# Moving, splitting and re-sharing the side jobs of a fused convolution and gated feed-forward kernel

## The chip, the cores and the metric

The kernel runs on one core of one Trainium2 chip. The metric is device time in microseconds (us): the median over runs of the whole program. Each set of runs of a kernel was made beside runs of the kernel before on the same chip. Profile spans are about 1.8 us shorter than the time of the same run.

The engines are TensorE (PE; its weight loads are PEld), VectorE (DVE), ScalarE (ACT), GpSimd (POOL) and the sync engine (SP), whose queue issues most of the transfers.

## The reference

```python
# attention part: weights w = softmax(weight) over 7 taps, one row for each of 8 heads of 24 channels
out[b, s, h] = sum_k w[h, k] * x[b, s - 6 + k, h]      # x: 8 x 4096 x 192, zeros before s = 0
# feed-forward part on the 32768 rows of out
g = out @ w_gate                                       # 192 x 1536
y = (silu(g) * (out @ w_val)) @ w_out                  # 1536 x 192
```

All inputs and the output are float32; the kernel works in fp16 with float32 sums.

## The kernel before

The program is one loop of 768 steps. Twelve steps make a block of 512 rows, four blocks (48 steps) a unit. The scheduler does not reorder within an engine: `seq` chains each engine's instructions in the order of their emission.

A step makes 512 rows of one 128-wide slice of gate and of val, each in its own bank of PSUM (the tiles from `ppool`, which the matmuls write). The banks come from rings of three, that is, three banks used in turn:

```python
def gate_val(n):
    g = ppool.tile([P, TB], fp32, tag="gate", ...)      # bufs=3
    v = ppool.tile([P, TB], fp32, tag="val", ...)       # bufs=3
    ...                                                 # three pairs of 64-row matmuls (PE)
    silu[n] = seq(nc.scalar.activation(sg, g, AF.Silu)).ins     # ACT
    seq(nc.vector.tensor_tensor(hj, sg, v, op=ALU.mult))        # DVE: h
```

At steps 1, 4, 7 and 10 of a block 12, 24 or 36 `down` matmuls on finished h follow. The convolution is made in two ways. Unit 1 and the even units from 2 on are convolved on PE by band matmuls (`conv_half`), at two steps of the unit before (10 and 22; 25 and 31 in unit 0), with banks from the same gate and val rings:

```python
for hp in (2 * hh, 2 * hh + 1):
    banks = [ppool.tile([P, TB], fp32, tag=tag, name="cv") for tag in ("gate", "val")]
    ...                                                 # 16 matmuls into them
```

Odd units from 3 on ("pooled" units) are convolved tap by tap in channel-major form, beside PE: six jobs a unit, each with seven taps, done in slots at steps 1, 7 and 10 of a block.

```python
ON_DVE, ON_ACT, ON_POOL = (0, 1), (2, 3, 4), (5, 6)
def step(a):                       # three slots a job
    if a < len(ON_DVE):
        on_dve(ON_DVE[a])          # total = x_k * tap + (0 or total)
    on_act(ON_ACT[a])              # part = x_k * tap on ACT; then total += part on POOL
    if a == len(ON_ACT) - 1:
        for k in ON_POOL:
            on_pool(k)             # POOL: piece = x_k * tap (tensor_scalar); total += piece
```

The x of these jobs is transposed by DMAs on the sync queue. Their taps per channel come from a small computation at step 23: iota on POOL, two small operations on DVE for each of two selectors (`pick`), then matmuls into gate banks (`ctap`). One more transfer matters later: for the band matmuls of unit 2, `dup_x` copies the lower rows of `x16` after step 37, on the same sync queue.

## Time and profile before

| | |
|---|---|
| median of three runs | 792.34 us (791.21 to 792.58) |
| span of the profiled run | 788.7 us |
| PE, DVE, ACT, POOL busy | 99%, 80%, 74%, 57% |
| a block far from the start | 11.73 us, with a band convolution 12.4 us |
| unit 0 (48 steps) by the starts of its gate matmuls | 60.46 us |

PE is never idle for more than a fraction of a microsecond except in unit 0 and at its border. The lines are in the prediction. A line of a timeline reads: start, duration, engine, source line, operation, output and inputs, shapes; a bracket at the end has the engine's idle time before it and what ended it. Source lines shift with the edit: in the changed kernel L767 is gate and val, L776 the silu, L778 h, L793 the down matmuls, L668 DVE's taps, L649 POOL's multiply, L634 its adds.

### The profile page before, as it was taken

How to read it: one execution, taken by the hardware profiler on the slowest of the kernel's cores; microseconds unless marked ns; L12 is line 12 of the kernel's file. 1: busy time of each engine (PE TensorE's matmuls, PEld its weight loads, DVE VectorE, ACT ScalarE, POOL GpSimd, SP SyncE). 2: the span in 40 equal slices, each digit the busy share in tenths (PEclk: the TensorE clock that was granted, in tenths of full speed). 3: DMA queues.
4: the chain of work that ended last, by engine and by line, in shares of the span. 5: the costliest groups of instructions: out<-in, count | busy, mean ns of one | idle time of the engine just before them, and what ended most of it. 6: DMA issues, size and time to landing. Idle time of an engine off the chain costs nothing.

```text
span 788.7 us, 28107 instructions
## 1 busy us (share of the span) xinstructions
PE 778.3 (99%) x11563; PEld 600.3 (76%) x11563; DVE 627.3 (80%) x988; ACT 584.7 (74%) x1010; POOL 453.3 (57%) x375
## 2 busy tenths in 40 slices
PE   8898999999999999999999999999999999999998
PEld 5665678886788767887678876888678886788886
DVE  7666888688887888778897788877888788897775
ACT  6566778678777787777787687777787777786664
POOL 8204669455793658926689166873669546684000
PEclk9999999999999999999999999999999999999999
DMA  9996668653585444853557625674257652531111
GB/s 144 152 165 130 136 134 149 136 109 80 111 151 124 94 108 102 168 118 62 129 116 135 137 63 118 129 152 110 56 134 135 145 117 59 119 93 44 42 42 42
DMA packets 175970, 88.49 MB, mean 112 GB/s; under 512 B 115898, under 2 KB 175170, under 8 KB 175170
## 3 DMA queue, kind: packets, MB, share of 16 engines
q1 hardware_dynamic: 147634, 69.57, 38.3%
q0 software_dynamic: 28208, 17.13, 16.4%
q8 instruction: 90, 1.47, 0.8%
q14 instruction: 38, 0.31, 0.1%
HBM read 34.26 MB, written 39.37 MB: 93 GB/s over the span
## 4 chain that ended last, share of the span: by engine, by line
PE 96%; SPq 1%; ACT 1%; DVE 0%; DMA 0%; issue 0%; ACTq 0%
PE gate L740 51%; PE acc L766 32%; PE val L740 11%; PE cv L462 1%; SPq L498 1%; PE warm L841 1%; SPq L520 0%; PE turn L431 0%; DMA x<-xs 0%; PE cv L373 0%; ACT sig L749 0%; PE acc L787 0%; DVE h L751 0%; ACT tme L391 0%; ACT wide L331 0%
## 5 line engine op out<-in xcount | busy, mean ns | idle before, releaser
L751 DVE TENSOR_TENSOR h<-sig,val 128x512 f16<-128x512 f16 x768 | 503.5, 686 | 144.9 <-PE val L740 93.6
L749 ACT ACTIVATE sig<-gate 128x512 f16<-128x512 f32 x768 | 458.2, 597 | 176.1 <-PE val L740 104.0
L740 PEld LDWEIGHTS <-w 64*128 64x128 f16 x4608 | 321.8, 110 | 125.4 <-issue 2.9
L766 PEld LDWEIGHTS <-h 64*128 64x128 f16 x6096 | 275.8, 94 | 45.7 <-issue 4.0
L766 PE MATMUL acc<-wo,h 64*128 64x192 f16 x6096 | 306.1, 243 | 2.1 <-ACT sig L749 2.1
L740 PE MATMUL val<-xc,w 64*128 64x512 f16 x1296 | 306.9, 378 | 0.0
L740 PE MATMUL gate<-xc,w 64*128 64x512 f16 x1296 | 306.9, 378 | 0.0
L636 POOL TENSOR_TENSOR total<-total,part 128x512 f32<-128x512 f32 x126 | 160.1, 1270 | 225.9 <-DVE total L619 174.1
L740 PE MATMUL val<-pxc,w 64*128 64x512 f16 x1008 | 236.6, 376 | 0.0
L740 PE MATMUL gate<-pxc,w 64*128 64x512 f16 x1008 | 236.6, 376 | 0.0
L649 POOL TENSOR_SCALAR piece<-x,tap_c 128x512 f32<-128x512 f16 x84 | 137.9, 1641 | 0.0
L643 ACT ACTIVATE part<-x,tap_c 128x512 f32<-128x512 f16 x126 | 89.9, 714 | 3.7 <-DMA x<-xs 3.1
L636 POOL TENSOR_TENSOR total<-total,piece 128x512 f32<-128x512 f32 x42 | 54.2, 1290 | 3.5
L619 DVE SCALAR_TENSOR_TENSOR total<-x,tap_c,fill 128x512 f32<-128x512 f16 x42 | 41.1, 979 | 2.4 <-DMA x<-xs 2.4
L636 POOL TENSOR_TENSOR pxc<-total,piece 128x512 f16<-128x512 f32 x28 | 36.1, 1288 | 2.3
L825 DVE COPY o_sb<-acc 128x384 f32<-128x384 f32 x63 | 34.6, 549 | 0.0
L619 DVE SCALAR_TENSOR_TENSOR total<-x,tap_c,total 128x512 f32<-128x512 f16 x42 | 31.4, 748 | 3.5 <-POOL total L636 3.5
L824 ACT COPY o_sb<-acc 128x384 f32<-128x384 f32 x63 | 30.2, 479 | 0.1
L98 POOL DMA_DIRECT2D x<-in_x_dram x25 | 19.8, 800 | 13.3 <-ACT sig L749 13.1
L479 ACT CAST tm<-cv 128x480 f16<-128x480 f32 x32 | 16.3, 562 | 11.8 <-PE cv L462 11.8
L479 DVE CAST tm<-cv 128x480 f16<-128x480 f32 x32 | 19.6, 652 | 1.2
L490 POOL COPY tm<-tm 128x1280 f16<-128x1280 f16 x8 | 10.0, 1249 | 17.3 <-DVE tm L479 9.1
(68 smaller groups left out, 101.0 us busy)
## 6 DMA issues: line engine op xcount, KB each, us to landing
out_dram<-o_sb SPq DMA_DIRECT2D x63, 384.0 KB
scr<-tm SPq DMA_DIRECT2D x56, 130.0 KB
x<-x SPq DMA_DIRECT2D x14, 480.0 KB
xs<-in_x_dram POOLq DMA_DIRECT2D x7, 774.0 KB, 7.3
x<-in_x_dram POOLq DMA_DIRECT2D x11, 480.0 KB, 7.8
pxc<-pxc SPq DMA_DIRECT2D x56, 64.0 KB
pxc<-y SPq DMA_DIRECT2D x56, 64.0 KB
x<-in_x_dram POOLq DMA_DIRECT2D x7, 468.0 KB, 6.0
```

Source lines behind the costliest of these rows:

```text
L98: nc.gpsimd.dma_start(out=t[p0 + i0 : p0 + i1, w0 - at : w1 - at, :], in_=bass.AP(tensor=x_flat.tensor, offset=(t0 + size * w0 - pad + i0) ...
L479: eng(tm[u][:, NG * r : NG * r + NG, 2 * grp * hp : 2 * grp * hp + 2 * grp].rearrange("p g (t e) -> p g t e", t=2), banks[r][:, 0 : 2 * w] ...
L619: nc.vector.scalar_tensor_tensor(total.rearrange("p (s e) -> p s e", s=SUBS) if k == 0 else total, shifted(k).rearrange("p (s e) -> p s e" ...
L636: nc.gpsimd.tensor_tensor(dst if k == K - 1 else total, total, part, op=ALU.add)
L643: seq(nc.scalar.activation(part, shifted(k), AF.Copy, scale=tap[:, k : k + 1]))
L649: nc.gpsimd.tensor_scalar(part, shifted(k), scalar1=tap[:, k : k + 1], scalar2=None, op0=ALU.mult,)
L740: nc.tensor.matmul(o, w16[m][p0 : p0 + Q, k, e::E], xc[b][k][p0 : p0 + Q, 0:TB], start=(k == 0), stop=(k == SL - 1),)
L749: silu[n] = seq(nc.scalar.activation(sg, g, AF.Silu)).ins
L751: seq(nc.vector.tensor_tensor(hj, sg, v, op=ALU.mult))
L766: nc.tensor.matmul(acc[b][bank][:, s, :], hj[p0 : p0 + Q, ts(2 * bank + s, P)], wo16[p0 : p0 + Q, j, :], start=(not second and j == 0 and ...
L824: seq(nc.scalar.copy(o_sb[:, 0:2, :], acc[b][0]))
L825: seq(nc.vector.tensor_copy(o_sb[:, 2:4, :], acc[b][1]))
```

## The change

Its intent is to take the side jobs out of PE's way at the start of the program and to balance them better. It has these parts:

1. **Taps in two steps.** The selectors are made after step 24, the `ctap` matmuls after step 33.
2. **First jobs later.** A pooled unit's jobs are queued 95 steps ahead of it (103 before), those of the first one 86 ahead.
3. **New shares.** Jobs alternate two and three taps on DVE (three and two on ACT). Each slot takes one DVE tap and one ACT tap, each from its own list, and POOL's adds of a job start only when all of its DVE taps have been issued.
4. **POOL multiplies by broadcast taps**, as a two-input operation.
5. More buffers for some tiles, fewer for others, and the halves of the tiles are placed later.

```diff
-    def make_channel_taps():
+    def make_picks():
 ...
+    def make_channel_taps():
+        for name in pick:
             bank = ppool.tile([P, TB], fp32, tag="gate", name="ctap")
 ...
-    ON_DVE, ON_ACT, ON_POOL = (0, 1), (2, 3, 4), (5, 6)
+    SHARES = (
+        ((0, 1), (2, 3, 4), (5, 6)),
+        ((0, 1, 2), (3, 4), (5, 6)),
+    )
 ...
+        def proceed():
+            if job["dve"]:
+                return
+            while job["parts"]:
+                add(*job["parts"].pop(0))
+            if job["act"]:
+                return
+            for k in pool_taps:
+                part = cpool.tile([P, TB], fp32, tag="piece", name="piece", bufs=2)
+                seq(nc.gpsimd.tensor_tensor(part, shifted(k),
+                        job["tap"][:, k : k + 1].to_broadcast([P, TB]), op=ALU.mult))
+                add(part, k)
 ...
-        plan.setdefault(s0 - 103, []).append(
-            lambda: pending.extend((v, *job) for job in jobs)
-        )
+        plan.setdefault(s0 - (86 if v == POOLED[0] else 95), []).append(lambda: queue_jobs(v))
 ...
     def pooled_work(n, room):
+        if room:
+            if on_dve:
+                on_dve.pop(0)()
+            if on_act:
+                on_act.pop(0)()
 ...
-        if n == 23:
+        if n == 24:
+            make_picks()
+        if n == 33:
             make_channel_taps()
```

More of the change, by code (lines that the diff above doesn't have):

```diff
@@ L532 @@
     taps = {}
-    def make_channel_taps():
+    pick = {}
+    def make_picks():
         for name, first, rows in (("c01", 0, P), ("c2", P, Q)):
@@ L546, in make_channel_taps @@
             seq(nc.vector.tensor_single_scalar(low, which, 0, op=ALU.is_ge))
-            pick = small(f"pick_{name}", [H, P], fp16)
+            pick[name] = small(f"pick_{name}", [H, P], fp16)
             seq(
                 nc.vector.scalar_tensor_tensor(
-                    pick, which, float(grp), low, op0=ALU.is_lt, op1=ALU.mult
+                    pick[name], which, float(grp), low, op0=ALU.is_lt, op1=ALU.mult
                 )
             )
+    def make_channel_taps():
+        for name in pick:
             bank = ppool.tile([P, TB], fp32, tag="gate", name="ctap")
@@ L556, in make_channel_taps @@
                     nc.tensor.matmul(
-                        bank[:, 0:K], pick, split[:, a, 0:K, 0],
+                        bank[:, 0:K], pick[name], split[:, a, 0:K, 0],
                         start=(a == 0), stop=(a == 1),
@@ L591, in turn_x @@
         tag = f"x{at // Q}"
-        t = cpool.tile([P, TB + XP], fp16, tag=tag, name=tag, bufs=4)
+        t = cpool.tile([P, TB + XP], fp16, tag=tag, name=tag, bufs=6)
         seq(nc.sync.dma_start_transpose(out=t, in_=rows[:, at : at + P]))
@@ L597, in join_x @@
         seq(nc.sync.dma_start(out=x12[u, i + 2][0:Q], in_=x12[u, i][Q:P]))
-    ON_DVE, ON_ACT, ON_POOL = (0, 1), (2, 3, 4), (5, 6)
-    def conv_job(u, what, i):
-        if what == "pair":
-            dst = y2[u, i] = cpool.tile([P, TB], fp16, tag="y2", name="y2", bufs=4)
-            src, tap = x12[u, i + 2], taps["c2"]
-        else:
-            t = cpool.tile([P, XW], fp16, tag="pxc0", name="pxc0", bufs=6)
-            xc[UB * u + i] = [t]
-            dst = t[:, 0:TB]
-            src, tap = x01[u, i], taps["c01"]
-        total = cpool.tile([P, TB], fp32, tag="total", name="total", bufs=3)
-        at = XP - pad
-        def shifted(k):
-            return src[:, at + k : at + k + TB]
-        def on_dve(k):
-            zero = fill.unsqueeze(1).to_broadcast([P, SUBS, P])
+    SHARES = (
+        ((0, 1), (2, 3, 4), (5, 6)),
+        ((0, 1, 2), (3, 4), (5, 6)),
+    )
@@ new lines, with conv_job, open_job, add @@
+    on_dve = []
+    on_act = []
+    finished = {}
+    started = []
+    def conv_job(n_job, u, what, i):
+        dve_taps, act_taps, pool_taps = SHARES[n_job % len(SHARES)]
+        job = {"dve": len(dve_taps), "act": len(act_taps), "parts": []}
+        at = XP - pad
+        def open_job():
+            if what == "pair":
+                y2[u, i] = cpool.tile([P, TB], fp16, tag="y2", name="y2", bufs=4)
+                job.update(dst=y2[u, i], src=x12[u, i + 2], tap=taps["c2"])
+            else:
+                t = cpool.tile([P, XW], fp16, tag="pxc0", name="pxc0", bufs=8)
+                xc[UB * u + i] = [t]
+                job.update(dst=t[:, 0:TB], src=x01[u, i], tap=taps["c01"])
+            job["total"] = cpool.tile([P, TB], fp32, tag="total", name="total", bufs=4)
+        def shifted(k):
+            return job["src"][:, at + k : at + k + TB]
+        def add(part, k):
+            total = job["total"]
+            seq(
+                nc.gpsimd.tensor_tensor(
+                    job["dst"] if k == K - 1 else total, total, part, op=ALU.add
+                )
+            )
+        def proceed():
[7 more added lines that the diff above has]
+                part = cpool.tile([P, TB], fp32, tag="piece", name="piece", bufs=2)
+                seq(
+                    nc.gpsimd.tensor_tensor(
+                        part,
+                        shifted(k),
+                        job["tap"][:, k : k + 1].to_broadcast([P, TB]),
+                        op=ALU.mult,
+                    )
+                )
+                add(part, k)
+            finished[u, what, i] = True
+        def dve_step(k):
+            if "total" not in job:
+                open_job()
+            total, x_k, other = job["total"], shifted(k), job["total"]
+            if k == 0:
+                total = total.rearrange("p (s e) -> p s e", s=SUBS)
+                x_k = x_k.rearrange("p (s e) -> p s e", s=SUBS)
+                other = fill.unsqueeze(1).to_broadcast([P, SUBS, P])
@@ L618, in on_dve @@
             seq(
                 nc.vector.scalar_tensor_tensor(
-                    total.rearrange("p (s e) -> p s e", s=SUBS) if k == 0 else total,
-                    shifted(k).rearrange("p (s e) -> p s e", s=SUBS)
-                    if k == 0
-                    else shifted(k),
-                    tap[:, k : k + 1],
-                    zero if k == 0 else total,
-                    op0=ALU.mult,
-                    op1=ALU.add,
-                )
-            )
-        def part_tile(name):
-            return cpool.tile([P, TB], fp32, tag=name, name=name, bufs=4)
@@ L634, in add @@
-        def add(part, k):
-            seq(
-                nc.gpsimd.tensor_tensor(
-                    dst if k == K - 1 else total, total, part, op=ALU.add
-                )
-            )
-        def on_act(k):
-            part = part_tile("part")
-            seq(nc.scalar.activation(part, shifted(k), AF.Copy, scale=tap[:, k : k + 1]))
-            add(part, k)
-        def on_pool(k):
-            part = part_tile("piece")
-            seq(
-                nc.gpsimd.tensor_scalar(
-                    part, shifted(k), scalar1=tap[:, k : k + 1], scalar2=None,
-                    op0=ALU.mult,
-                )
-            )
-            add(part, k)
@@ L656, in step, with act_step @@
-        def step(a):
-            if a < len(ON_DVE):
-                on_dve(ON_DVE[a])
-            on_act(ON_ACT[a])
-            if a == len(ON_ACT) - 1:
-                for k in ON_POOL:
-                    on_pool(k)
-        return [lambda a=a: step(a) for a in range(len(ON_ACT))]
+                    total, x_k, job["tap"][:, k : k + 1], other,
+                    op0=ALU.mult, op1=ALU.add,
+                )
+            )
+            job["dve"] -= 1
+            proceed()
+        def act_step(k):
+            if "total" not in job:
+                open_job()
+            part = cpool.tile([P, TB], fp32, tag="part", name="part", bufs=6)
+            seq(
+                nc.scalar.activation(
+                    part, shifted(k), AF.Copy, scale=job["tap"][:, k : k + 1]
+                )
+            )
+            job["act"] -= 1
+            job["parts"].append((part, k))
+            proceed()
@@ L666, in place @@
+        on_dve.extend(lambda k=k: dve_step(k) for k in dve_taps)
+        on_act.extend(lambda k=k: act_step(k) for k in act_taps)
     def place(u, i):
@@ L669, in place @@
             xc[b].append(
-                cpool.tile([P, XW], fp16, tag=f"pxc{k}", name=f"pxc{k}", bufs=6)
+                cpool.tile([P, XW], fp16, tag=f"pxc{k}", name=f"pxc{k}", bufs=4)
             )
@@ L685, with queue_jobs @@
     plan = {}
-    pending = []
-    started = []
-    finished = set()
+    jobs_made = []
     placing = []
+    def queue_jobs(u):
+        for what, i in (
+            ("block", 0), ("pair", 0), ("block", 1), ("pair", 1),
+            ("block", 2), ("block", 3),
+        ):
+            conv_job(len(jobs_made), u, what, i)
+            jobs_made.append((u, what, i))
+        placing.extend((u, i) for i in range(UB))
     def planned(v):
@@ L700, in planned @@
             plan.setdefault(s0 + off, []).append(lambda i=i: join_x(v, i))
-        jobs = [("block", 0), ("pair", 0), ("block", 1), ("pair", 1)]
-        jobs += [("block", 2), ("block", 3)]
-        plan.setdefault(s0 - 103, []).append(
-            lambda: pending.extend((v, *job) for job in jobs)
-        )
-    def pooled_work(n, room):
-        while room:
-            if not started:
-                if not pending:
-                    break
-                u, what, i = pending.pop(0)
-                started.append((u, what, i, conv_job(u, what, i)))
-            u, what, i, steps = started[0]
-            steps.pop(0)()
-            room -= 1
-            if not steps:
-                started.pop()
-                finished.add((u, what, i))
-                for q in range(UB):
-                    need = {(u, "block", q), (u, "pair", q % 2)}
-                    if need <= finished and (u, what, i) in need:
-                        placing.append((n + 14, u, q))
-        while placing and placing[0][0] <= n:
-            _, u, q = placing.pop(0)
-            place(u, q)
+        plan.setdefault(s0 - (86 if v == POOLED[0] else 95), []).append(lambda: queue_jobs(v))
+    def pooled_work(n, room):
+        if room:
[3 more added lines that the diff above has]
+                on_act.pop(0)()
+        while placing:
+            u, i = placing[0]
+            need = (u, "block", i), (u, "pair", i % 2)
+            for job in need:
+                if finished.get(job) is True:
+                    finished[job] = n
+            if not all(job in finished for job in need):
+                break
+            if n < max(max(finished[job] for job in need) + 12, ustep * u + NCH * i - 16):
+                break
+            placing.pop(0)
+            place(u, i)
     hbuf = {}
@@ L895 @@
             job()
-        pooled_work(n, 0 if work else {1: 1, 7: 1, 10: 1}.get(j, 0))
+        pooled_work(n, j in (1, 7, 10) and not work)
         if u + 1 < NU and not pooled(u + 1):
```

## The prediction

> **What bounds the kernel now.** I read the page first. It names TensorE:
>
> ```profile
> PE 778.3 (99%) x11563; PEld 600.3 (76%) x11563; DVE 627.3 (80%) x988; ACT 584.7 (74%) x1010; POOL 453.3 (57%) x375
> ...
> PE 96%; SPq 1%; ACT 1%; DVE 0%; DMA 0%; issue 0%; ACTq 0%
> ```
>
> A busy PE is not proof of a PE at its peak, since the ends of matmuls are modelled. So I compared starts. The program has 768 steps (three gate/val matmul pairs, then a silu on ScalarE and a product h on VectorE); twelve make a block, 48 a unit. From the starts of h, every block from 84 us on takes 11.73 us, or 12.4 us in the two blocks of a unit in which TensorE also makes a convolution, until the last. Pairs start 0.215 us apart. The change removes and adds no matmul, so in this stretch nothing can be gained. Unit 0 and its border alone hold waits, and the table of busy times by stretch shows them:
>
> ```profile
> 35.95:39.37 3.42, 1.33 (x18) 0.62 (x16) 1.61 (x6) 0.76 (x2) 1.03 (x3) 1.00 0.99 102
> 39.37:42.78 3.41, 3.41 (x24) 1.55 (x24) 0.80 (x2) 1.36 (x3) 0.00 (x0) 0.50 1.71 128
> 63.25:66.67 3.42, 1.32 (x24) 0.81 (x22) 1.47 (x3) 1.95 (x4) 1.04 (x1) 1.00 0.51 112
> 66.67:70.08 3.41, 3.41 (x34) 2.26 (x30) 1.83 (x3) 1.18 (x3) 1.48 (x2) 0.50 0.64 86
> 551.83:563.56 11.73, 11.73 (x197) 8.51 (x194) 10.24 (x16) 9.18 (x16) 7.42 (x6) 1.00 0.28 54
> ```
>
> After the window come its length, then the busy time of PE, PEld, DVE, ACT and POOL; the third number from the end is the granted clock. Twice PE is busy for only 1.3 of 3.4 us, and twice the next 3.41 us run at clock 0.50. Each stop thus costs its idle time and half of a 3.41 us window, 1.7 us, on top. The last line is one steady block: VectorE has 1.5 us of slack in it.
>
> The first stop, from the timeline (start, duration, engine; in brackets the idle time before and its cause):
>
> ```profile
> 36.46 0.38 PE L740 MATMUL val<-xc,w 64*128 64x512 f16 x1
> ...
> 37.50 0.69 DVE L751 TENSOR_TENSOR h<-sig,val 128x512 f16<-128x512 f16 x1 [1.45 <-ACT sig L749]
> ...
> 38.34 0.28 DVE L549 SCALAR_TENSOR_TENSOR pick_c<-which_c,low_c 8x128 f16<-8x128 int32 x1
> ...
> 38.68 0.21 PE L556 MATMUL ctap<-split,pick_c 8*128 8x7 f16 x2 [1.85 <-DVE pick_c L549]
> ...
> 39.27 0.59 PE L740 MATMUL gate<-xc,w 64*128 64x512 f16 x1
> ```
>
> The ctap matmuls stand in PE's order behind step 23, but need selectors (pick) that VectorE makes only after h of step 23. The second stop:
>
> ```profile
> 63.50 0.38 PE L740 MATMUL val<-xc,w 64*128 64x512 f16 x1
> 64.72 0.72 ACT L643 ACTIVATE part<-x,tap_c 128x512 f32<-128x512 f16 x1 [3.14 <-DMA x<-xs]
> ...
> 65.35 1.55 ACT L749 ACTIVATE sig<-gate 128x512 f16<-128x512 f32 x3
> ...
> 65.98 2.45 PE L766 MATMUL acc<-wo,h 64*128 64x192 f16 x36 [2.10 <-ACT sig L749]
> ```
>
> The first channel-major job is queued at step 43, before its transposed x has landed. ScalarE runs in order, so the next silu sits behind the tap, and PE behind the silu.
>
> [...] Durations are minimum/median/maximum:
>
> ```profile
> L619 DVE SCALAR_TENSOR_TENSOR total<-x,tap_c,fill x42: 744/747/1409, 64.7 to 703.5; 128x512 f32<-128x512 f16 x42
> L619 DVE SCALAR_TENSOR_TENSOR total<-x,tap_c,total x42: 744/748/753, 67.8 to 708.9; 128x512 f32<-128x512 f16 x42
> ```
>
> First taps are 0.75 us or, 15 times, 1.39 to 1.41. Second taps are never slowed, because in this kernel GpSimd waits for them. One slow one:
>
> ```profile
> 584.43 1.27 POOL L636 TENSOR_TENSOR total<-total,piece 128x512 f32<-128x512 f32 x1
> ...
> 584.86 1.39 DVE L619 SCALAR_TENSOR_TENSOR total<-x,tap_c,fill 128x512 f32<-128x512 f16 x1
> ...
> 585.67 2.00 POOL L649 TENSOR_SCALAR piece<-x,tap_c 128x512 f32<-128x512 f16 x1
> ...
> 586.17 1.27 DVE L751 TENSOR_TENSOR h<-sig,val 128x512 f16<-128x512 f16 x2
> ...
> 586.90 0.37 PE L740 MATMUL val<-pxc,w 64*128 64x512 f16 x1
> ```
>
> The tap met an add with 0.84 us to go and lost 0.65 us; the next GpSimd multiply (usually 1.56) was held in turn. That h ends at 586.84 and the val matmul that needs its bank starts at 586.90, barely 0.05 us late and with no loss of pace: in this place (a tap after a step of remainder 1 in its block) 1.40 us is just what PE does not feel. [...] the adds here take 1.27. I take 1.27 for the multiply by broadcast taps; no run shows it yet.
>
> **The change, part by part.**
>
> *Taps in two steps.* From the start of step 23 (36.02) to that of step 26 (43.91) go 7.89 us. Unhindered, two steps of 0.65 and one with a convolution (2.40, as at step 31) are 3.70, so the stop costs 4.19. It does not vanish whole. Selectors now come after h of step 24: four small operations, together 0.95 us by their starts (38.10 to about 39.05). In step 25 two convolution pairs take two of the three gate and val banks, so val of step 26 needs the bank of h of step 25. That h would end at about 39.5 and now ends at about 40.4, against a PE ready at 39.7: 0.7 lost. At step 33 the two ctap banks take the same ring: gate of step 34 needs the bank of step 33, whose silu ends 0.79 after PE has finished step 33 (52.13 against 51.34 in the trace), plus a signal of 0.05: 0.84 lost. Neither leaves a window mostly idle, so I expect no clock drop. Net: 4.19 - 0.70 - 0.84 = 2.65 gained.
>
> *First jobs later.* Steps 46 to 49 take 7.37 us (63.07 to 70.44) where 2.13 + 0.65 + 0.65 = 3.43 would do: 3.94. The first job now waits for step 58, which itself holds a convolution, so really step 61. The x tile landed at 64.7; step 61 starts about 77. I expect all 3.94.
>
> *Two and three taps in turn.* Each slot (steps 1, 7 and 10 of a block) now has one VectorE and one ScalarE tap, so six jobs need 15 slots, not 18. VectorE gains 21 taps of 0.75 or more (105 for 84), ScalarE loses 21 of 0.71, GpSimd 21 adds of 1.27. A steady block with three taps costs VectorE, back to back, 12 x 0.60 + 0.53 + 3 x 0.75 = 10.0 us; with every tap at 1.40 it is 11.9 against 11.73. So the sum fits unless all are blocked. The local limit is the slot at step 1. Taps no longer wait for GpSimd's adds, so more of them meet GpSimd busy. Counting slots, about two of the step-1 slots of a unit fall in a busy stretch, 14 in seven units. A tap that meets an add at a random point waits up to about 1.07 us, 0.42 over the limit at worst; averaged over the 1.27 us this is about 0.1, and with lag carried from the slot before I take 0.15: 14 x 0.15 = 2 lost.
>
> *GpSimd.* Multiplies go from 1.64 mean to about 1.27: 84 x 0.37 = 31 us less work, all beside PE. More tile buffers and later placing take waits from queues that PE does not wait for.
>
> Sum: 792.3 - 2.65 - 3.94 + 2 = 787.7. The new slots were presumably tuned by someone who looked at the clock, so I lean a little lower: 787.0.
>
> **The rivals.**
> 1. *Contention decides.* GpSimd's stream is now all two-input work, and phases repeat from unit to unit, so a bad phase at step 1 repeats seven or fourteen times: 14 x 0.42 = 6 us, or 792; with lag over whole stretches, 35 blocks x 0.3 = 10 us, or 796. For it: the lines at 584.43. Against: the 1.5 us of slack.
> 2. *The transfers become the bound.* Without the stops PE reaches unit 1 some 6 us sooner. Its first x comes by the sync queue (last transpose issued at 60.8, landing near 63.4), which starts after the convolution of step 31 and so moves 3.5 us forward: near 60. Step 48 would start at 69.5 - 6.3 = 63.2. It holds by 3 us; if the queue did not move at all, 0.2 us and a little more would be lost, near 788.
> 3. *Clean gain.* If the two small stops of steps 26 and 34 overlap better than I think and no phase is bad: 792.3 - 8.1 = 784.2.
> 4. *GpSimd falls behind* (multiply of 2 us or more) and ScalarE waits for part buffers. A job then has 4.5 adds and two multiplies, 9.7 us, in the 10.9 or so that a job has with skipped slots. Unlikely; 795 or more.
>
> **Range and chances.** The gain is bounded by the 8.1 us of the two stops, 1.0%: faster by 2% (776.5) has no source. Slower by 2% (808) needs some 22 us of new stalls, 0.5 us in each of some 40 blocks; possible only if rival 1 or 4 is strong. Low is rival 3, 784; high is rival 1, 794.
>
> **What would show it.** Right: no ctap gap of 1.9 us; no tap waiting for a transposed x near 64 us; no window at clock 0.50 between 5 us and the end; small gaps before the val matmul of step 26 and the gate matmul of step 34, of 0.7 to 0.8 us; later taps on VectorE at up to 1.8 us; GpSimd multiplies at about 1.27. Wrong: blocks after 100 us that take more than 11.73 or 12.4 us by over 0.3, PE waiting for h in the steady part, or a new wait of PE on a transfer at step 48.

## The result, and the profile after

The changed kernel takes 787.62 us, the median of four runs (787.03 to 790.05), beside 792.46 for the kernel before. A ratio in this document is the mean time of one kernel's fast runs over that of the other's of the same rounds, so not quite the ratio of the medians quoted. Here it is 0.9945, with a 95% interval of 0.9918 to 0.9971: about half a per cent faster. The profiled run has a span of 785.3 us, 3.4 less than before.

The page of the changed kernel, its busy times and its chain:

```profile
PE 776.7 (99%) x11563; PEld 560.8 (71%) x11563; DVE 662.5 (84%) x1009; ACT 572.2 (73%) x989; POOL 392.3 (50%) x354
...
PE 95%; SPq 3%; DMA 1%; ACT 0%; DVE 0%; issue 0%; ACTq 0%
```

The counts of DVE (988 to 1009) and ACT (1010 to 989) show the 21 taps that moved; POOL has 61 us less to do. PE is still the bound. What is new in the chain is 3% for the sync queue and 1% for a DMA.

**The first stop** has become two small ones. At step 26:

```profile
39.60 0.28 DVE L551 SCALAR_TENSOR_TENSOR pick_c<-which_c,low_c 8x128 f16<-8x128 int32 x1
...
39.80 0.67 DVE L778 TENSOR_TENSOR h<-sig,val 128x512 f16<-128x512 f16 x1
39.87 0.38 PE L767 MATMUL gate<-xc,w 64*128 64x512 f16 x1
...
40.53 0.37 PE L767 MATMUL val<-xc,w 64*128 64x512 f16 x1 [0.28 <-DVE h L778]
```

The gate matmul of step 26 goes ahead at 39.87, its val partner waits until h of step 25, put off by the selectors, is done at 40.47. And at step 34:

```profile
47.92 0.30 PE L561 MATMUL ctap<-split,pick_c 8*128 8x7 f16 x4
...
48.52 0.23 ACT L567 COPY tap_c<-ctap 128x7 f32<-128x7 f32 x2
48.67 0.37 PE L767 MATMUL gate<-xc,w 64*128 64x512 f16 x1 [0.45 <-ACT tap_c L567]
```

The profile puts the wait of this gate matmul down to `tap_c`. But in the order of the ring its bank is that of step 33, whose silu ended at 48.62, 0.05 before the matmul began, while the first `tap_c` copy ended only at 48.67. So it is the silu, as the prediction has it.

From start to start of the gate matmuls, steps 23 to 26 now take 3.69 us (7.89 before), step 26 takes 0.48 more than a free step, step 33 takes 0.84 more, and step 31 0.05 more. So of the 4.19 us of the first stop 1.37 are left.

**The second stop is gone**: steps 46 to 49 take 3.43 us, as they should. No window has clock 0.50 between 5.8 us and the last microseconds of the profiled run.

**A new wait came at step 58**, in the timeline:

```profile
73.89 0.27 PE L462 MATMUL cv<-x,band 64*32 64x240 f16 x1
...
75.81 0.60 PE L462 MATMUL cv<-x,band 64*32 64x240 f16 x31 [1.64 <-DMA x<-x]
```

The band convolution for unit 2 waits for `dup_x`, the copy of the lower rows. PE arrives 6.6 us sooner than before (step 58 starts at 72.1, before at 78.7), the copy is issued only 2.7 us sooner (68.08, before 70.75). The wait costs 1.95 us.

**DVE's taps** meet POOL more often, and for longer (minimum/median/maximum of each group):

```profile
L668 DVE SCALAR_TENSOR_TENSOR total<-x,tap_c,total x63: 737/940/1809, 85.6 to 705.4; 128x512 f32<-128x512 f16 x63
L668 DVE SCALAR_TENSOR_TENSOR total<-x,tap_c,fill x42: 743/993/1820, 80.2 to 696.6; 128x512 f32<-128x512 f16 x42
```

Before, 15 of 84 taps were over 0.81 us and none over 1.41. Now 60 of 105 are over 0.81, and 19 over 1.41. Nearly all of that is hidden. What shows is 0.21 us at the second band convolution of each odd unit from 3 to 13 (unit 15 makes none); one of the six, from 561 us:

```profile
561.05 1.04 POOL L649 TENSOR_TENSOR piece<-x,tap_c 128x512 f32<-128x512 f16 x1
...
562.17 1.27 POOL L634 TENSOR_TENSOR pxc<-total,piece 128x512 f16<-128x512 f32 x1
...
562.25 1.75 DVE L668 SCALAR_TENSOR_TENSOR total<-x,tap_c,total 128x512 f32<-128x512 f16 x1
...
563.92 1.87 DVE L778 TENSOR_TENSOR h<-sig,val 128x512 f16<-128x512 f16 x3
...
564.83 0.80 PE L462 MATMUL cv<-x,band 64*32 64x240 f16 x32
```

The tap after step 19 begins 0.08 us after an add and stands behind nearly all of it. The products of steps 20 and 21 come late. The convolution takes two banks of each ring, and the second pair still belongs to step 21, so the 32 matmuls, 0.60 us when nothing holds them, take 0.80. By the starts of steps, step 22 of the odd units 3 to 13 takes 0.20 to 0.21 us more than before, 1.25 in all.

The sum, by profile: -2.82 for the first stop, -3.94 for the second, +1.95 at step 58, +1.2 in the odd units, and 0.1 at the start make -3.5, against -3.4 for the spans.

### The profile page after: what moved, and what is told of

It is laid out like the page before. It is cut to its first block, busy times and chain, and to the rows that moved or that the text cites.

```text
span 785.3 us, 28098 instructions
## 1 busy us (share of the span) xinstructions
PE 776.7 (99%) x11563; PEld 560.8 (71%) x11563; DVE 662.5 (84%) x1009; ACT 572.2 (73%) x989; POOL 392.3 (50%) x354
## 4 chain that ended last, share of the span: by engine, by line
PE 95%; SPq 3%; DMA 1%; ACT 0%; DVE 0%; issue 0%
PE gate L767 55%; PE acc L793 31%; PE val L767 6%; PE cv L462 1%; SPq L520 1%; DMA x<-x 1%; SPq L498 1%; SPq L598 1%; PE warm L868 1%; PE turn L431 0%; PE cv L373 0%; PE acc L814 0%; DVE h L778 0%; ACT tm L479 0%; ACT tme L391 0%
## 5 line engine op out<-in xcount | busy, mean ns | idle before, releaser
L767 PEld LDWEIGHTS <-w 64*128 64x128 f16 x4608 | 287.2, 110 | 155.2 <-issue 1.9
L793 PEld LDWEIGHTS <-h 64*128 64x128 f16 x6096 | 266.6, 94 | 51.2 <-issue 3.4
L793 PE MATMUL acc<-wo,h 64*128 64x192 f16 x6096 | 300.8, 243 | 0.0
L634 POOL TENSOR_TENSOR total<-total,part 128x512 f32<-128x512 f32 x105 | 141.5, 1347 | 254.5 <-DVE total L668 236.4
L649 POOL TENSOR_TENSOR piece<-x,tap_c 128x512 f32<-128x512 f16 x84 | 96.3, 1147 | 0.0
L681 ACT ACTIVATE part<-x,tap_c 128x512 f32<-128x512 f16 x105 | 75.0, 715 | 0.0
L668 DVE SCALAR_TENSOR_TENSOR total<-x,tap_c,total 128x512 f32<-128x512 f16 x63 | 68.6, 1089 | 0.0
L668 DVE SCALAR_TENSOR_TENSOR total<-x,tap_c,fill 128x512 f32<-128x512 f16 x42 | 44.0, 1048 | 0.0
```

The lines of the kernel that those rows point to most:

```text
L634: nc.gpsimd.tensor_tensor(job["dst"] if k == K - 1 else total, total, part, op=ALU.add)
L649: nc.gpsimd.tensor_tensor(part, shifted(k), job["tap"][:, k : k + 1].to_broadcast([P, TB]), op=ALU.mult,)
L668: nc.vector.scalar_tensor_tensor(total, x_k, job["tap"][:, k : k + 1], other, op0=ALU.mult, op1=ALU.add,)
L681: nc.scalar.activation(part, shifted(k), AF.Copy, scale=job["tap"][:, k : k + 1])
L767: nc.tensor.matmul(o, w16[m][p0 : p0 + Q, k, e::E], xc[b][k][p0 : p0 + Q, 0:TB], start=(k == 0), stop=(k == SL - 1),)
L793: nc.tensor.matmul(acc[b][bank][:, s, :], hj[p0 : p0 + Q, ts(2 * bank + s, P)], wo16[p0 : p0 + Q, j, :], start=(not second and j == 0 and ...
```

## The experiments

Twelve runs, all correct. "Span" is that of the profiled run; compare it with 788.7 (before) and 785.3 (changed). Medians compare best within one call of three or four kernels, which shares the runs of the kernel before. Gains rest on the intervals that leave out 1. Spans carry scatter too: the first step starts between 8.8 and 9.6 us, and at 9.13 and 9.42 in the two profiles of the changed kernel.

| run | span | median | before beside it | ratio (95%) |
|---|---|---|---|---|
| ctap_only | 788.4 | 790.44 | 791.43 | 0.9980 (0.9954 to 1.0006) |
| late_only | 791.1 | 792.11 | 791.43 | 1.0009 (0.9985 to 1.0032) |
| stops_only | 787.4 | 789.33 | 791.43 | 0.9977 (0.9952 to 1.0001) |
| dup_early | 783.6 | 785.54 | 791.43 | 0.9923 (0.9904 to 0.9942) |
| skip_tap | 787.1 | 788.56 | 792.00 | 0.9952 (0.9929 to 0.9975) |
| first_early | 788.0 | 789.47 | 792.00 | 0.9967 (0.9951 to 0.9982) |
| pool_scalar | 788.5 | 791.29 | 792.00 | 0.9988 (0.9964 to 1.0012) |
| best | 781.2 | 783.45 | 792.00 | 0.9896 (0.9879 to 0.9913) |
| best_old_shares | 783.3 | 784.91 | 793.04 | 0.9902 (0.9885 to 0.9920) |
| stops_free | 785.8 | 787.58 (one run) | 793.04 | none |
| after_again | 785.8 | 788.60 | 793.04 | 0.9954 (0.9934 to 0.9975) |
| best_free | 781.5 | 782.89 | 791.55 | 0.9899 (0.9882 to 0.9915) |

### ctap_only: the taps in two steps, alone

```diff
 # in the kernel before: make_channel_taps split as in the change
-        if n == 23:
+        if n == 24:
+            make_picks()
+        if n == 33:
             make_channel_taps()
```

> The kernel before with one part of the change alone: selectors after step 24, tap matmuls after step 33. My theory: the first stop (4.2 us) shrinks to two small ones of about 0.47 us at step 26 and 0.84 us at step 34, so the span falls by 2.7 to 2.9 us; the second stop near step 46 stays, with its window at clock 0.50. Rival (moving the taps only moves the stop): a PE gap of over 1.5 us at ctap, and a span within 1 us of before.

The small stops at steps 26 and 34 are those of the changed kernel, gap for gap, so the first stop is explained. The rest missed: the span fell by 0.3 us only. PE now reaches the jobs sooner, and their data do not come as much sooner. The next lines are the ACT taps of the first and of the second job:

```profile
61.95 0.72 ACT L648 ACTIVATE part<-x,tap_c 128x512 f32<-128x512 f16 x1 [2.74 <-DMA x<-xs]
...
76.17 0.72 ACT L648 ACTIVATE part<-x,tap_c 128x512 f32<-128x512 f16 x1 [3.36 <-DMA x<-x]
```

The first stops PE for 1.9 us, without a half-clock window this time. The second, which had waited 0.6 us before, stops it for about 2.4 us, and a window at clock 0.50 follows. The gain of the part is real where it is made and is given back where the next transfer is met.

### late_only: the first jobs later, alone

```diff
-        plan.setdefault(s0 - 103, []).append(
+        plan.setdefault(s0 - (86 if v == POOLED[0] else 103), []).append(
```

> The kernel before with only the first pooled unit's jobs queued at step 58 instead of 41. Theory: the stop at step 46 (3.9 us) goes, but the sync queue has not moved forward, so the copy of x's lower rows that the convolution of step 58 needs lands about 78.4 us while PE asks for it at about 76.4: a new PE wait of 1.7 to 2.2 us, and a span only 1.7 to 2.3 us shorter. Rival (the step-58 wait of the changed kernel comes from the new shares of taps): no wait there, 3.9 us shorter.

The wait at step 58 came, and larger:

```profile
76.83 0.27 PE L462 MATMUL cv<-x,band 64*32 64x240 f16 x1
...
79.38 0.60 PE L462 MATMUL cv<-x,band 64*32 64x240 f16 x31 [2.28 <-DMA x<-x]
```

So it does not come from the new shares. But the kernel is not shorter at all: the wait (2.5 us) pulls a window at clock 0.50 behind it (1.7), 0.5 us are lost at step 48 on a transposed x, and near 132 and 164 us come two waits of 1.4 and 0.4 us, of which the next run explains the first. Removing a stop of 3.9 us alone gained nothing.

### stops_only: both, with the old shares

Edit: the two diffs above together.

> The kernel before with both of these, but with its old shares of taps, three slots a job and the old GpSimd multiply. Theory: both stops go as in the changed kernel and the wait of 1.9 us at step 58 is there too, but the convolution at step 22 of the odd units loses nothing, so the span is 1.0 to 1.4 us shorter than that of the changed kernel (784.0 or so in the profile against 785.3). Rival (the new shares are what makes the gain possible): longer than the changed kernel's.

Both stops went and the wait of step 58 came, as expected. The odd units from 3 on took 48.20 to 48.26 us, against 48.41 to 48.47 in the changed kernel: that loss is the price of the new shares. But the span was 2.1 us longer than the changed kernel's, not shorter, for two reasons. The wait at step 58 was followed by a window at clock 0.50. And this came near 129 us:

```profile
125.32 2.36 POOL L98 DMA_DIRECT2D x<-in_x_dram  x3
...
127.69 1.29 POOL L641 TENSOR_TENSOR total<-total,part 128x512 f32<-128x512 f32 x1
...
129.01 0.75 DVE L624 SCALAR_TENSOR_TENSOR total<-x,tap_c,total 128x512 f32<-128x512 f16 x1 [2.71 <-POOL total L641]
...
130.42 0.34 PE L771 MATMUL acc<-wo,h 64*128 64x192 f16 x4 [1.21 <-DVE h L756]
```

With the old order DVE's second tap needs POOL's first add. POOL is busy issuing loads, DVE waits for the add, h waits behind the tap in DVE's order, and PE waits for h. It costs PE 1.4 us by the starts of its matmuls. In the kernel before, the jobs lay 17 steps earlier, and the longest such wait of DVE was 0.6 us. So here the rival was nearer: something in the new job code is what lets the first jobs start late.

### dup_early: the copy of the lower rows sooner

```diff
-            if ls == (37 if u == 0 else 26):
+            if ls == (32 if u == 0 else 26):
                 dup_x(u + 2)
```

> The changed kernel with the copy of unit 2's lower rows issued after step 32 instead of step 37. Theory: the wait of PE at step 58 (1.9 us) is the place of that copy in the sync queue, so it goes without a new one: 1.8 to 2.0 us shorter than the changed kernel, 783.4 in the profile. Rival (the copy is slow because the transfers are saturated): it still lands late or holds up the transposes behind it, and less than 1 us is gained.

The span is 783.6 us, as expected, and the median 785.54. The convolution of step 58 runs in one piece:

```profile
74.15 0.60 PE L462 MATMUL cv<-x,band 64*32 64x240 f16 x32
```

A wait of 0.2 us for a transposed x appeared at step 48. The place of the copy in the queue was the cause. All four runs lie between 784.78 and 785.62, with a mean clock of 0.999 or 1.000.

### skip_tap: no DVE tap ahead of the second convolution

```diff
-            if on_dve:
+            if on_dve and n % (2 * ustep) != ustep + 19:
                 on_dve.pop(0)()
```

> The changed kernel, but VectorE takes no tap in the slot after step 19 of the odd units, just ahead of the convolution of step 22. Theory: the tap there is held by a GpSimd add for 1.0 us (1.75 to 1.79 us long), the products of steps 20 and 21 come late, and the second pair of banks of the convolution waits for them, 0.21 us in each of six units. So that loss goes: six times 0.21, 1.2 to 1.3 us shorter than the changed kernel (784.0 in the profile), unless the taps put off by one slot meet a new bad phase. Rival (the loss comes from ScalarE or the casts): step 22 still takes 2.97 us in the odd units.

The 0.21 us at step 22 went in all six units. The taps put off met a new bad phase: in units 5 to 13 the first convolution (step 10) took 0.06 to 0.10 us more than in the changed kernel, so an odd unit took 48.33 instead of 48.47. The mechanism held, the gain was 0.9 us instead of 1.25. The span grew all the same, by 1.8 us, because the wait of step 58 was 0.6 longer this time and was followed by a half-clock window. One of its four runs had none: 785.89 us at mean clock 1.000, the others 788.2 to 789.7 at 0.998.

### first_early: all jobs queued at the same distance

```diff
-        plan.setdefault(s0 - (86 if v == POOLED[0] else 95), []).append(lambda: queue_jobs(v))
+        plan.setdefault(s0 - 95, []).append(lambda: queue_jobs(v))
```

> The changed kernel with the first unit's jobs queued at step 49 like all others' (with the new shares the first slot is then step 49, about 65 us). Theory: the data decide. The first block's x lands about 61.5 us, before that slot; the joined tile of the pair is asked for at step 61, after the convolution of step 58, so also later than it lands: no new wait, span within 0.5 us of the changed kernel, and the special case of the first unit earns nothing by itself. Rival (the later first job is what removes the second stop): PE waits 1 us or more near step 49 or 52 behind a tap that waits for a transfer.

No tap waited for a transfer and PE lost nothing between steps 46 and 57, so 95 steps ahead is late enough even for the first unit. The span missed: it is 2.7 us longer, 0.8 by a longer wait at step 58 and most of the rest by the window behind it. Its copy of the lower rows was issued 0.8 us later than in the changed kernel (68.89 against 68.08). That can be ordinary scatter: in skip_tap, which is the same program as the changed kernel up to step 67, the wait was 0.6 us longer, and in the repeated changed kernel 0.26. Whether the earlier jobs add to it is open.

### pool_scalar: the old multiply on GpSimd

```diff
-                    nc.gpsimd.tensor_tensor(
-                        part, shifted(k), job["tap"][:, k : k + 1].to_broadcast([P, TB]), op=ALU.mult)
+                    nc.gpsimd.tensor_scalar(
+                        part, shifted(k), scalar1=job["tap"][:, k : k + 1], scalar2=None, op0=ALU.mult)
```

> The changed kernel with GpSimd's old multiply by a scalar operand. Theory: GpSimd is off the path, so about 35 us more of its time (84 multiplies at 1.56 for 1.15) moves the span by less than 1.5 us, through the phases at which its adds meet VectorE's taps. Rival (GpSimd falls behind without the faster multiply): ScalarE or VectorE wait for its buffers and the span grows by over 2 us.

This missed: the span grew by 3.2 us. The multiply took 1.68 us in the mean (1.15 in the changed kernel), 45 us in all. DVE and ACT do not wait for POOL's buffers, so the rival's way is not seen. Instead the phases moved to the place that the prediction had named as the limit, a slow tap after step 1 and val of step 5 behind it:

```profile
201.40 1.59 DVE L666 SCALAR_TENSOR_TENSOR total<-x,tap_c,fill 128x512 f32<-128x512 f16 x1
...
202.92 1.27 DVE L776 TENSOR_TENSOR h<-sig,val 128x512 f16<-128x512 f16 x2
...
203.12 0.38 PE L765 MATMUL gate<-pxc,w 64*128 64x512 f16 x1
...
203.65 0.37 PE L765 MATMUL val<-pxc,w 64*128 64x512 f16 x1
```

The gate matmul has its bank at 203.12; val, which usually starts beside it, comes 0.53 us later. Step 5 loses about 0.35 us in each of six units, 2.1 in all, while the loss at step 22 falls away in most. And once, at step 156, PE waits 0.9 us for tiles placed late. Apart from 0.2 us at step 58 and 0.3 before the first step, the broadcast multiply thus earned 2.7 us, most of the net gain of the change, by the phases and by earlier ends of jobs; no engine was short of POOL's time on average.

### best: four small edits to the changed kernel

```diff
-            if on_dve:
+            if on_dve and n % (2 * ustep) != ustep + 19:
 ...
-        if n == 24:
+        if n == 14:
             make_picks()
-        if n == 33:
+        if n == 34:
             make_channel_taps()
 ...
-            if ls == (37 if u == 0 else 26):
+            if ls == (34 if u == 0 else 26):
```

> The changed kernel with four small edits: no VectorE tap after step 19 of the odd units, the copy of unit 2's lower rows after step 34, selectors after step 14, tap matmuls after step 34 (behind the long run of down matmuls). Theory: minus 1.9 for the copy, 1.26 for the tap, 0.47 for the selectors, about 0.65 for the banks: 781.0 in the profile, or up to 781.7 if PE then reaches unit 1 before its first transposed x has landed. Rival (transfers bound the first units): 782.5 or more, the gains turned into waits at steps 48 and 60.

The span is 781.2 us, inside the expectation. The median is 783.45, ratio 0.9896: faster than both kernels, and its interval does not touch that of the changed kernel. At step 14 h has slack, so the selectors cost nothing; after step 34 the 36 down matmuls cover the ring of gate banks, and only 0.3 us is left there, the time of the tap matmuls themselves. Unit 0 takes 52.93 us (54.05 in the changed kernel), unit 1 48.20 (50.15).

### best_old_shares: the same places, old shares

Edit: stops_only with the last three edits of the version above.

> The kernel before with both stops removed and the three edits of the best version that are not about shares (copy after step 34, selectors after step 14, tap matmuls after step 34), but old shares, three slots a job. Theory: the waits that the old shares bring to a late first job stay, 1.2 us near 129 us where a VectorE tap waits for a GpSimd add that stands behind the issue of loads, and 0.2 near 161 us where a tap waits for its x; the steady units are exact. So it is about 1.4 to 1.8 us slower than an exact schedule and within 1 us of the best version (781.2). Rival (the new shares earn more than they cost): over 1.5 us slower than the best version. Other rival (they cost more): over 0.5 us faster.

The span is 783.3 us: unit 2 takes 1.96 us too long (1.4 at 124 us behind an add, 0.6 at 157 us behind a late x), the odd units 48.25 where the best version has 48.34. By profile it is 2.1 us slower than the best version, of which 0.4 lie before the first step; by the starts of the gate matmuls 1.6. So the rival that the new shares earn more than they cost is right here, if barely: its limit was 1.5. The timed ratios (0.9902 and 0.9896) cannot separate the two.

### stops_free: POOL's adds after both DVE taps, old shares

```diff
-            add(part, k)
+            held.append((part, k))
 ...
             on_act(ON_ACT[a])
+            while a > 0 and held:
+                add(*held.pop(0))
```

> The kernel with both stops removed and the old shares, but GpSimd's adds of a job are issued only after both of its VectorE taps, as the new shares do it. Theory: the wait of 2.7 us of the second tap for GpSimd near 129 us, and PE's 1.2 us behind it, go; in exchange second taps meet GpSimd's adds and some take up to 1.8 us (in the old order none over 0.76). Rival (that wait comes from the three slots a job): it stays.

Only the one profiled execution was taken, so its state is unknown and the trace alone is read. The wait of 2.7 us and PE's behind it went: the order of the adds, not the number of slots, was the cause. The second half of the expectation was wrong in the good direction:

```profile
L624 DVE SCALAR_TENSOR_TENSOR total<-x,tap_c,fill x42: 744/746/784, 82.1 to 700.5; 128x512 f32<-128x512 f16 x42
L624 DVE SCALAR_TENSOR_TENSOR total<-x,tap_c,total x42: 744/746/747, 87.5 to 705.9; 128x512 f32<-128x512 f16 x42
```

No tap of 84 is held by POOL for more than 0.04 us. That is not because POOL is done: 36 of the 42 first taps begin while it still works on the job before. But 30 of them fall into its one-input multiply with at most 1.12 us to go, and 6 into the last 0.2 us of an add, and none of these is held for more than the same 0.04 us. The last section has such taps in the kernel before, where they were not delayed either. Odd units from 3 on take 48.20 us, less than in the kernel before.

### after_again: the changed kernel once more

> The changed kernel once more, beside these. Theory: [...] runs fall near 787.3 (mean clock 0.999) or near 789.5 (0.997 or 0.998), with little between. Rival: a continuous spread with no tie to the clock.

The runs were 787.60 (mean clock 0.999), 788.64, 788.55 and 789.32 (0.997 to 0.998). With the four of the first set (787.03, 787.46 and 787.78 at 0.999, 790.05 at 0.997) every run at 0.999 is below 787.8 and every run at 0.997 or 0.998 above 788.5. The tie to the clock holds; two tight groups, as expected, they are not, since the second is 1.5 us wide. What decides whether a run has a half-clock window is not shown; among the profiled runs here, the longer waits at step 58 were the ones with a window behind them (see the last section).

### best_free: old shares, adds after both taps, all places mended

Edit: best_old_shares with the edit of stops_free and the first jobs 95 steps ahead.

> Old shares (two VectorE taps, three slots a job, old GpSimd multiply) with GpSimd's adds issued only after both VectorE taps, the first unit's jobs queued from step 49, selectors after step 14, tap matmuls after step 34, the copy of unit 2's lower rows after step 34. Theory: no VectorE tap is longer than 0.8 us, odd units with convolutions take 48.20 us exactly, no wait near 129 or 160 us, so the profile shows 780.5 to 781.0, as short as the best version or 0.2 to 0.7 us shorter: the new shares are not needed for the gain. Rival (three slots a job end too late for the next unit's loads): a wait of 0.2 to 1 us near 125 or 160 us stays, 781.3 or more.

The span is 781.5 us and the median 782.89. The steady units are exact (48.20 and 46.92 us) and no wait is left near 125 or 160 us. Still the span lies above the 781.0 that was expected, for PE now comes to step 48 before its first transposed x:

```profile
63.33 0.37 PE L749 MATMUL gate<-xc,w 64*128 64x512 f16 x1 [0.43 <-DMA xc<-scr]
```

That costs 0.6 us, and the runs scatter between 782.3 and 783.4. It equals the best version within the measurement: from the first step to the start of unit 15 the two take 719.46 and 719.45 us. So neither the alternating shares nor the broadcast multiply are needed for this time.

## Why the prediction was right or wrong

The total came true: 787.0 forecast, 787.62 measured, and well inside the range. Its steps did so only in part, and the total was helped by luck: by profile the change brought 3.4 us, and the prediction's own sum was 4.6. The profiled run of the kernel before (790.49) happened to be one of its faster runs, its median being 792.46.

- **PE bounds, and only unit 0 has anything to give.** Right. The even units have the length of before to 0.01 us.
- **Taps in two steps: 4.19 lost before, 0.70 and 0.84 left.** Right in mechanism at both places. The second measured 0.84. The first measured 0.48: h of step 25 ended at 40.47, as forecast, but only val waits for it, and the pairs behind make up part of the gap between val and gate. Net 2.82 instead of 2.65.
- **No clock drop from the small stops.** Right: the clock record has 1.00 from 5.8 to 784.0 us. The slowest of the four timed runs (790.05 us at mean clock 0.997) probably had a half-clock window, behind the wait of step 58; it was not profiled.
- **First jobs later: all 3.94.** Right for the stop itself (a slip aside: the first job is queued at step 41, and 43 is its first slot). The term is only worth that together with other places: late_only gained nothing.
- **New shares: 2 us lost to contention at the step-1 slots, 14 times 0.15.** The cause was right, down to the longest tap (1.82 us against a bound of 0.75 + 1.07). The place was wrong: PE lost 0.21 us in six units at the convolution of step 22, where a tap at step 19 delays the products whose banks the convolution takes. 1.2 us instead of 2 (the mean excess, taken as about 0.1, works out to 0.07). So PE waiting for h in the steady part, one of the signs of being wrong, came true in this small form. The working looked at gate and val rings for ordinary steps and forgot that a convolution draws four banks at once and so shortens the slack, although the same working used that for step 26. The step-1 place is real: pool_scalar loses 0.35 us there six times over.
- **GpSimd's multiply at 1.27.** It is faster: 1.04 us alone, 1.15 in the mean. That it lies "all beside PE" was wrong as a statement about worth: it changes the phases, and going back cost 2.7 us (pool_scalar).
- **Rival 2, the transfers.** This is the step that failed. The margin was computed for step 48 alone, and there it held. But the sync queue has other customers: the copy for the convolution of step 58 stands behind it. Its 64 packets of 15360 bytes can be told apart in the packed traces: in the kernel before the last ended at 76.65 and PE asked at 80.47; in the changed kernel it ended at 75.02, and PE asked at 73.89 and went on at 75.81. So the copy landed 1.6 us sooner, and PE asked 6.6 us sooner. The 1.95 us there were in no term. The prediction's sign of being wrong, a new wait of PE on a transfer, came true, only at step 58 and not 48. dup_early shows the cause: the copy moved five steps ahead, and the wait is gone.
- **More buffers and later placing.** Not tested alone. No wait of PE on these tiles is in the changed kernel.
- **Why part 3 is there at all** was not seen. Its worth is not the balance of taps but that DVE no longer waits for POOL within a job, which a late start of the jobs would have exposed (stops_only, 1.4 us). stops_free shows that this can be had without new shares and without contention.

## What to carry to other kernels

When the bound engine is paced as evenly as PE here (the even units kept their length to 0.01 us), list every consumer of each queue that works in order before taking a stop away: what lands later than PE now arrives is the next stop, and it can be a transfer unrelated to the edit, like the copy on the sync queue that cost 1.95 us at step 58. Small setup work belongs where the ring of banks has slack or right ahead of a long run of matmuls that needs none of them (in best the selectors cost nothing, the tap matmuls 0.3 us); and an engine that works in order and feeds the bound one should not wait, within a side job, for a third engine that also issues loads (2.71 us of waiting on DVE, 1.4 us lost on PE in stops_only). Two engines that hold each other up, as DVE and POOL do here (a tap of 0.75 us took up to 1.82), and run in a fixed rhythm can repeat the same collision in every period (0.20 to 0.21 us in each of six odd units), so a change that only shifts the rhythm can earn or cost microseconds (2.7 in pool_scalar).

## What the traces show of the clock and of GpSimd

- **Half-clock windows.** The clock record of the kernel before has two stretches at clock 0.50 between the program's start and end, from 39.36 and from 66.67 us, each 3.413 us long; the changed kernel's has none. Ahead of the two, PE was busy for 1.33 and 1.32 of 3.4 us, with one wait of 1.85 and one of 2.10 us. In stops_only 1.23 of 3.41 us busy were followed by clock 0.50. In the changed kernel 1.77 of 3.41 us busy, around the wait of step 58, were not:

```profile
73.13:76.54 3.41, 1.23 (x45) 0.74 (x39) 0.86 (x3) 0.18 (x2) 0.00 (x0) 1.00 0.70 132
76.54:79.95 3.41, 3.41 (x31) 1.83 (x26) 1.50 (x3) 1.56 (x3) 1.25 (x1) 0.50 0.69 174
```

```profile
74.04:77.45 3.41, 1.77 (x50) 1.22 (x51) 1.40 (x3) 1.02 (x2) 0.00 (x0) 1.00 0.60 100
```

  The first two lines are of stops_only, the third of the changed kernel; the columns are those of the stretches in the prediction. In skip_tap and first_early the wait of step 58 was 0.6 and 0.8 us longer than in the changed kernel and a half-clock window followed, so a little more waiting did cost about 1.7 us on top (half of 3.41, an estimate). Where the limit lies is not shown.
- **Taps on DVE beside GpSimd** (times to go are by GpSimd's recorded spans). In the kernel before, 7 taps that began with 0.17 to 0.20 us of an add (1.27 us) to go took no longer than 0.75 us, and 15 with 0.84 to 0.86 to go took 0.65 to 0.66 longer. In the changed kernel 66 began with 0.23 to 1.26 us of an add to go and took 0.04 to 1.08 longer. The one-input multiply (1.56 us) of the kernel before had 0.38 to 0.46 us to go when 13 taps began, and none was delayed; with 0.39 to 0.45 us of an add to go, taps of the changed kernel took 0.20 to 0.25 longer. Three taps began in the last 0.15 us of the multiply by broadcast taps (1.04 us) and were not delayed; how long it holds a tap that begins sooner is not shown by these two traces.
- **GpSimd's own times.** For 128x512 the one-input multiply of fp16 by a scalar per partition took 1.56 us (kernel before), the two-input multiply by broadcast taps 1.04 (changed kernel) and a two-input float32 add 1.27 (both); from its start to that of the next instruction, where no tap is in the way, at least 1.64, 1.11 and 1.21. So here the multiply with two inputs was the faster one.
